# One copy per value tile and per turned attention tile, a state step that stores no minimum, and a new written order

## The chip, the cores and the metric

The kernel runs on one core of one Trainium2 chip. The metric is the device time of one execution in microseconds (us). The kernel before took 319.63 us (median of 3 runs, 318.43 to 320.39).

## The reference

Two stages follow each other. The first is a linear recurrence with decay over 4 batches, 8 heads, 768 steps and head size 48. With a state of 48 x 48 per head, each step computes

```
y[t]  = r[t] @ (state + outer(u*k[t], v[t]))
state = w[t][:, None]*state + outer(k[t], v[t])
```

The heads' outputs side by side are rows x of 384 numbers. The second stage takes them through four experts (E = 4, head size 64). Each expert is causal attention over the 768 positions of a batch (`q = x@wq`, `k = x@wk`, `v = x@wv`, softmax of `0.125*q@k.T`), followed by its own output matrix `wo`. Gate logits `x@w_gate` choose two experts per position, and their outputs are added with softmax weights of the two logits.

## The kernel before, in words

The work is cut into 8 units: batch b = 0..3, half g = 0..1 of the positions (384 each). For every unit there is a recurrence part (`rwkv`) and an attention part (`moe`).

**Recurrence.** The positions are cut into chunks of 64, six per half, and the heads into four pairs p. Scans on VectorE form the products of decays, elementwise work on VectorE and GpSimd (POOL) scales k and r, and TensorE makes all sums in a chunk. What joins the chunks is the state step: `grow` (L435 to L449) computes for chunk c `ys[c+1] = (increment + ys[c]) * decay`, 112 partitions x 48 columns. The increment is in PSUM; the decay is one number per partition. The steps of one pair p form a chain of five or six. Two pairs are handled together (except in the very first unit), so the written order can alternate two chains. The step with chunk index 5 writes `wend` by a plain addition (L441), and for g = 0 the first step is a scaling (L447, L449). The other 144 steps use one VectorE instruction that adds, scales and also takes a minimum over the columns. That minimum goes to a tile `least` of one column, which every step shares and nothing reads:

```
nc.vector.tensor_tensor_reduce(out=new, in0=inc, in1=old, scale=by,
    scalar=3.0e38, op0=ALU.add, op1=ALU.min, accum_out=least[0:112])
```

**Attention.** `proj` makes queries and keys (L696 and L703), `vproj` makes for each 128 positions a row block of 260 columns in one PSUM bank (L735, L741): 128 value columns for experts 0 and 1, 128 for experts 2 and 3, and 4 gate logits. Three copies take these out: to `v_sb0`, to `v_sb1` and to `lg`. `scores` makes masked scores (L808), a row minimum of their negative on VectorE (L819) and exp on ScalarE (L824). `transposes` turns each attention row tile by TensorE, in 128 x 128 blocks, into two PSUM banks. The turned tile of position block ii (0 to 5 in a batch) has ii+1 blocks. The first four go to a tile `ATa` and a fifth and sixth to a tile `ATb`, so the tiles with ii = 4 and 5 are taken out by two copies (helper `copy`, L255 on ScalarE and L257 on VectorE). `attend` multiplies them with the values (L866), `weigh` scales by the gates, and `project_out` applies `wo` (L934) and stores.

**Order.** Nothing is scheduled at run time. The function `rwkv_moe` adds some 2,150 operations to a list, each with the engines that can do it. `ORDER` is a written list of engine letter and operation number (A ScalarE, V VectorE, P TensorE, G GpSimd, S the queue that issues all DMAs, SP); each engine runs its own entries in that order. Waits follow from the tiles that operations really read and write. [...] `P5` to `P98` are matmuls on zeros that fill TensorE at the start; 33 of them are in the list. TensorE runs in four tilings. Full 128-row matmuls (modes F and N) are one, 64 x 64 quarters (Q: recurrence) another, 64 rows (S and T: scores, transposes) a third and 64 columns (V: attention times values) the fourth. A transpose in mode T is two half blocks; where the entry ahead was a full matmul it is done as one full block instead (N).

Of the kernel before, what the change touches and what calls it, by code (L numbers as in the profile page):

```python
# [10 lines left out]

F32 = mybir.dt.float32
# [10 lines left out]
NT = S // 128  # L23
# [187 lines left out]
def rwkv_moe(ctx: ExitStack, tc: tile.TileContext, wkr, wkr0, vY, nat, uN, uT,  # L211
# [78 lines left out]
    least = cst.tile([128, 1], F32, name="least")  # L290
# [36 lines left out]
    def weights(n, src, cols, parts=1):  # L327

        f = sb([128, cols], F32, "ATa", f"w_{n}")
# [14 lines left out]
    def rwkv(b, g, v0, v1):  # L344
# [54 lines left out]
        def keys(group, n):  # L399
# [24 lines left out]
            for x, (p, kt, kts, vn, na, suf, sfv, ys) in enumerate(group):  # L424
# [10 lines left out]
                for c in range(NH - g):  # L435
                    i, a = divmod(c, 2)

                    def grow(e, c=c, o=columns(x, a, i), end=end, ys=ys, sfv=sfv):
# [5 lines left out]
                        if g or c:  # L444
                            nc.vector.tensor_tensor_reduce(out=new, in0=inc, in1=old, scale=by, scalar=3.0e38, op0=ALU.add, op1=ALU.min, accum_out=least[0:112])  # L445
# [214 lines left out]
    def moe(b, g, v0, v1):  # L660
# [6 lines left out]
        if g == 0:  # L667
# [3 lines left out]
            BT["v"] = [sb([128, NT, 128], F32, f"v_sb{ep}", f"v_sb{b}{ep}") for ep in range(2)]  # L671
# [4 lines left out]
        lg = sb([128, 3, E], F32, "lg", f"lg{n0}")  # L676
# [49 lines left out]
        def vproj(i):  # L726
            vp = bank(1, f"vp{n0}{i}")
            o = slice(i * 128, (i + 1) * 128)
            for k in range(3):
                step(0.333)  # L730
                if first:
# [4 lines left out]
                    plan.add("vproj", {"PE": 440}, mm, [(xh, kk) for kk in range(3)] + [wf] + ([vp] if k else []), [vp], claim=v_sb)  # L736
# [5 lines left out]
                plan.add("vproj", {"PE": 356}, mm, [(x_, kk) for x_ in (xh, xl) for kk in range(3)] + [("wh", "vg", 0), ("wl", "vg", 0)] + ([vp] if k else []), [vp],  # L742
                         claim=v_sb)
            for ep in range(2):
                plan.add("v", evac(128), lambda e, ep=ep: copy(e, v_sb[ep]()[:, 3 * g + i, :], vp()[:, ep * 128:ep * 128 + 128]),
                         [vp], [(v_sb[ep], 3 * g + i)])
            plan.add("lg", {"DVE": 70, "ACT": 100}, lambda e: copy(e, lg()[:, i, :], vp()[:, 256:260]), [vp], [(lg, i)])

        def gates():
# [5 lines left out]
            lgk = [(lg, i) for i in range(3)]  # L755
# [74 lines left out]
        def transposes(AT, a, x, i):  # L830
# [6 lines left out]
            plan.add("tp", {"PE": 62 * (ii + 1)}, tr, [a], [tp], mode="T", alt=109 * (ii + 1), claim=AT[0:1 + ii // 4])  # L837
            for j0 in range(0, ii + 1, 4):
                nj = min(4, ii + 1 - j0)

                def ev(e, j0=j0, nj=nj):
                    src = turned(tp, ii + 1)[:, j0:j0 + nj]
                    if j0 == 4:
                        dst = AT[1]()[:, (ii - 4) * 128:(ii - 4 + nj) * 128].rearrange("p (j h c) -> p j h c", j=nj, h=2)
                    else:
                        dst = AT[0]()[:, j0:j0 + nj, i * 128:(i + 1) * 128].rearrange("p j (h c) -> p j h c", h=2)
                    copy(e, dst, src)
                plan.add("ev", evac(nj * 128), ev, [tp], [(AT[j0 // 4], i)])
# [5 lines left out]
        def attend(ep, ATs, i0, i1):  # L854
# [3 lines left out]
            for j in range(nj):  # L858
# [3 lines left out]
                def mm(e, j=j, ia=ia, lo=lo, hi=hi):  # L862
                    for e in range(2):
                        at = ATs[e][j // 4]()
                        at = at[:, j, lo:hi] if j < 4 else at[:, lo - 128:hi - 128] if j == 4 else at[:, 256:384]
                        nc.tensor.matmul(yp()[e * 64:e * 64 + 64, lo:hi], v_sb[ep]()[:, j, e * 64:e * 64 + 64],  # L866
# [3 lines left out]
                         [(v_sb[ep], j)] + [(ATs[e][jj], i) for e in range(2) for i in range(i0, i1) for jj in range(g + 1)  # L870
                                            if 3 * g + i >= jj * 4] + ([yp] if j else []), [yp], mode="V")
# [70 lines left out]
        for ep in range(2):  # L942
            for qk in range(2):
                proj(ep, qk)
            if ep == 0:
                for i in range(3):
                    vproj(i)
                gates()
            ATs = [(sb([128, 4, 384], F32, "ATa", f"ATa{n0}{ep}{e}"),
                    sb([128, 384], F32, "ATb", f"ATb{n0}{ep}{e}") if g else None) for e in range(2)]  # L950
# [49 lines left out]
    for o in plan.order(dict(PE=7200.0 - 216 * WARM[0], DVE=3000.0, ACT=1700.0, POOL=3000.0, SP=1800.0)):  # L1000
# [11 lines left out]
        if e in BOTH and o["kind"] in BOTH[e]:  # L1012
# [10 lines left out]
BUFS = dict(lt=4, nat=3, ys=4, vy=3, suf=4, w2=3, pre=4, am=4, kt=4, rk=2, kts=4, xn=2, xh=2, xl=2, lg=2, asum=2, ge=2, m1=2, rank=2, c1=1, c2=1,  # L1023
            gs=2, mx=6, a=5, gg=2, gT=2, g3=2, yr=2, yh0=1, yh1=1, yl0=1, yl1=1, ob=3, v_sb0=1, v_sb1=1, ATa=3, ATb=2,
# [15 lines left out]
V327 A313 S287 V1082 V1093 G103 V1091 G356 V322 V328 V323 V329 V324 A1094 V330 V284 A314 S403 P1099 P1097 P1064 V283 P1060 G335  # L1040
A1083 P1070 A1085 V368 V1102 V1100 P1065 A1063 P1086 V374 V359 A0 P1071 A1062 A1061 A1101 P1066 P1072 V375 A1103 V406 V369 A1074 V357
V1075 P1088 A1067 V358 A1092 A1089 A1068 A1069 A1087 S480 V373 P336 A1098 V407 G360 A1073 V338 S465 P1104 V337 P1095 A1105 V106 P1106
P345 A1096 V1076 A1107 P378 A346 P342 A343 P394 V347 V344 G1077 S404 A379 A380 V395 V397 A361 G411 A1078 S107 G420 G413 P1108
P381 V376 P339 P1119 V1120 P1109 A340 V1122 V341 A377 V1079 S418 V421 V408 V472 A388 A1121 P1110 P1128 P1137 V1138 A382 V389 V1131
P1175 A1149 P1176 G414 P1179 A362 V383 S365 P1124 V1129 V390 P1177 P1180 V384 A1132 V391 A1178 V422 P1181 S466 P1183 G1080 V392 A1130
P1184 G425 G468 A1125 P1133 G412 A1182 A108 V1140 A1123 V385 V386 V393 V387 V423 P1206 P1135 V428 A1136 A1141 V424 V488 S534 A1134
P1185 V469 V427 V483 G429 G426 A1139 A1187 V1207 S350 P1215 P1243 V415 G474 V1216 A1208 P1142 P1244 A1188 V1218 P1189 A1186 P1195 V1151
V470 A1143 A1217 G476 P1126 P432 P1245 A1219 P1190 V1127 P1191 P448 V484 V471 A434 V487 V473 A433 V1209 V485 G1152 G489 V451 A1246
P435 V449 A1194 P399 A416 V436 G109 V442 V437 V400 V438 A430 V443 S481 V401 A1193 V439 V444 P1153 S519 V440 S419 P1144 A1192
V445 V441 A1154 V446 A1145 V447 A431 G537 G475 A1210 P1196 P1197 P1155 P1226 V1156 V1227 P1223 A1157 A1224 V1229 P1146 P1147 A1198 G477  # L1050
A505 A1200 P1148 P1220 A1199 G1158 A1225 V542 A499 S582 V486 V491 A1230 V538 V490 V522 A1150 V541 P495 V523 A496 P1247 A497 V1201
# [152 lines left out]
```

## Time and profile before

| | us |
|---|---|
| median of 3 runs | 319.63 |
| profiled execution | 319.12 |
| its span, first to last instruction | 317.3 |
| PE (TensorE) busy | 305.6 |
| DVE (VectorE) busy | 271.8 |
| ACT (ScalarE) busy | 243.1 |
| POOL (GpSimd) busy | 127.1 |

Sums below are made against the profiled execution of 319.12 us; 1.8 us of it lie around its span, and it is 0.5 us below the median of the runs. In the rows, PE is matmuls, PEld the loads of weights into TensorE, L12 a line of the kernel before. Matmuls overlap, so that a busy PE can still be waiting for part of the time.

### The profile page before, as it was taken

What the parts mean: (1) busy time and instruction counts of PE and PEld (TensorE: products, weight loads), DVE (VectorE), ACT (ScalarE), POOL (GpSimd) and SP (SyncE); (2) the same over time, 40 slices, a digit from 0 to 9 for tenths busy, and PEclk for the clock granted to TensorE, in tenths of its full rate; (3) what the DMA queues carried; (4) which work ended last, traced back from release to release, by engine and by line L of the source; (5) the groups of instructions that cost most, each with busy time, mean ns of one, the idle gap of its engine ahead of it and who ended that gap; (6) DMA issues with size and microseconds to landing.
All of it is one profiled execution on the core that took longest, in us unless ns stands there. A gap on an engine that the chain in (4) does not pass through costs nothing.

```text
span 317.3 us, 13468 instructions
## 1 busy us (share of the span) xinstructions
PE 305.6 (96%) x5304; PEld 248.4 (78%) x5304; DVE 271.8 (86%) x1001; ACT 243.1 (77%) x881; POOL 127.1 (40%) x252
## 2 busy tenths in 40 slices
PE   6979999999999999999999999999999999999995
PEld 2657667788776998898788978799889977888684
DVE  6999899999999999989998989998778766567852
ACT  1568978999899999998898786577678536677852
POOL 2123433567345454745656843475321010130330
PEclk9999999999999999999999999999999999999999
DMA  7998983762767466677166382341001002001012
GB/s 253 276 244 239 240 222 94 206 172 65 177 185 171 131 197 151 192 178 184 37 169 195 112 208 65 96 141 48 2 27 50 4 0 76 0 27 53 4 50 99
DMA packets 17759, 39.98 MB, mean 126 GB/s; under 512 B 2592, under 2 KB 10528, under 8 KB 17696
## 3 DMA queue, kind: packets, MB, share of 16 engines
q1 hardware_dynamic: 17696, 39.13, 44.7%
q8 instruction: 41, 0.67, 0.9%
q14 instruction: 22, 0.18, 0.2%
HBM read 34.40 MB, written 4.72 MB: 123 GB/s over the span
## 4 chain that ended last, share of the span: by engine, by line
PE 80%; DVE 11%; DMA 4%; issue 2%; ACT 1%; POOL 1%; SPq 0%; DVEq 0%; POOLq 0%; ACTq 0%
PE ps L703 14%; PE ps L808 12%; PE ps L866 11%; PE ps L934 8%; PE ps L251 7%; PE ps L741 7%; PE ps L247 5%; PE ps L613 4%; PE ps L376 3%; PE ps L422 3%; PE ps L378 3%; DMA nat<-in_nat_dram 2%; DVE ys L445 2%; DMA lt<-in_wkr_dram 2%; PE ps L735 1%
## 5 line engine op out<-in xcount | busy, mean ns | idle before, releaser
L824 ACT ACTIVATE a<-a,mx 128x128 f32<-128x128 f32 (+5 forms) x96 | 64.4, 673 | 4.9 <-DVE mx L819 4.3
L819 DVE CUSTOM_DVE_ANT_0 a<-ps,causal 128x256 f32<-128x256 f32 (+5 forms) x96 | 57.6, 619 | 11.7 <-PE ps L808 6.3
L445 DVE CUSTOM_DVE_ANT_0 ys<-ps,ys,suf 112x48 f32<-112x48 f32 x144 | 37.9, 263 | 4.0 <-DVE least L445 0.5
L255 ACT COPY ATa<-ps 128x512 f32<-128x512 f32 (+3 forms) x69 | 32.5, 484 | 11.5 <-PE ps L251 9.6
L866 PE MATMUL ps<-ATa,v_sb 128*64 128x384 f32 (+2 forms) x240 | 35.2, 430 | 0.0
L586 ACT ACTIVATE xn<-nat,rk 128x48 f32<-128x48 f32 x132 | 32.0, 331 | 0.1
L808 PE MATMUL ps<-K,Q 64*128 64x384 f32 (+4 forms) x160 | 31.7, 421 | 0.4 <-DVE xn L396 0.4
L703 PE MATMUL ps<-xh,wh_qk 128*128 128x384 f32 x84 | 31.9, 380 | 0.0
L703 PE MATMUL ps<-xl,wh_qk 128*128 128x384 f32 x84 | 28.4, 338 | 0.0
L703 PE MATMUL ps<-xh,wl_qk 128*128 128x384 f32 x84 | 28.3, 337 | 0.0
L866 PEld LDWEIGHTS ps<-ATa,v_sb 128*64 128x64 f32 x240 | 15.3, 136 | 12.7 <-issue 9.9
L251 PEld LDWEIGHTS ps<-ident,a 64*128 64x128 f32 x492 | 20.7, 138 | 5.6 <-issue 1.1
L376 PE MATMUL ps<-vy,am 64*64 64x48 f32 x768 | 24.8, 219 | 0.1
L378 PE MATMUL ps<-ys,pre 64*64 64x48 f32 (+1 forms) x704 | 24.4, 219 | 0.1
L251 PE MATMUL ps<-ident,a 64*128 64x64 f32 x492 | 23.9, 226 | 0.3 <-DVE least L445 0.2
L255 ACT COPY kts<-ps 128x384 f32<-128x384 f32 x30 | 13.6, 483 | 12.6 <-PE ps L247 9.1
L378 PEld LDWEIGHTS ps<-ys,pre 64*64 64x64 f32 (+1 forms) x704 | 21.9, 134 | 1.7 <-ACT xn L586 0.5
L558 POOL TENSOR_TENSOR kt<-lt,suf 128x384 f32<-128x384 f32 x21 | 19.6, 939 | 8.0 <-DVE w L551 3.8
L376 PEld LDWEIGHTS ps<-vy,am 64*64 64x64 f32 x768 | 22.6, 134 | 0.2 <-DVE am L618 0.2
L808 PEld LDWEIGHTS ps<-K,Q 64*128 64x128 f32 x160 | 15.5, 186 | 7.3 <-issue 2.7
L577 ACT ACTIVATE nat<-nat 128x48 f32<-128x48 f32 x90 | 20.6, 240 | 0.1
L554 POOL TENSOR_TENSOR lt<-lt 128x192 f32<-128x192 f32 x14 | 7.9, 561 | 31.3 <-DVE suf L547 14.9
(164 smaller groups left out, 933.9 us busy)
## 6 DMA issues: line engine op xcount, KB each, us to landing
lt<-in_wkr_dram SPq DMA_DIRECT2D x56, 218.6 KB, 4.5
nat<-in_nat_dram SPq DMA_DIRECT2D x28, 432.0 KB, 4.0
vy<-in_vY_dram SPq DMA_DIRECT2D x32, 144.0 KB, 3.6
out_dram<-ob SPq DMA_DIRECT2D x24, 192.0 KB, 1.9
lt<-in_wkr_dram SPq DMA_DIRECT2D x3, 583.0 KB, 6.0
w_qk<-in_wqk_dram SPq DMA_DIRECT2D x1, 768.0 KB, 8.1
nat<-in_nat_dram SPq DMA_DIRECT2D x4, 144.0 KB, 5.6
w_vg<-in_wvg_dram SPq DMA_DIRECT2D x1, 390.0 KB, 6.5
```

Source lines behind the costliest of these rows:

```text
L251: nc.tensor.transpose(o()[:, h * 512 + i * 64:h * 512 + i * 64 + 64], src[r], ident[r, r])
L255: nc.scalar.copy(o, i)
L376: nc.tensor.matmul(to, am()[k, c, :], vy()[k, c, :], start=zero and x == 0, stop=not first and i == 2 and x == len(group) - 1)
L378: nc.tensor.matmul(to, pre()[r, c, 0:C], ys()[r, c, :], start=i == x == 0, stop=False)
L445: nc.vector.tensor_tensor_reduce(out=new, in0=inc, in1=old, scale=by, scalar=3.0e38, op0=ALU.add, op1=ALU.min, accum_out=least[0:112])
L586: nc.scalar.mul(xn()[:, i, (2 * p + h) * D:(2 * p + h + 1) * D], v()[:, i, h, :], rk()[:, i, h:h + 1])
L703: nc.tensor.matmul(pp()[:, 0:384], w[:, qk, k, cs], x()[:, k, :], start=(k == j == 0), stop=(k == j == 2))
L808: nc.tensor.matmul(spv(x)[:, h, :], q_()[p, t], flat(k_())[p, o], start=j == 0, stop=j == len(terms) - 1)
L819: nc.vector.tensor_tensor_reduce(out=a()[:, 0:n].rearrange("p (a n) -> p a n", a=np_), in0=spv(x), in1=causal[:, S - n:S].rearrange("p (a ...
L824: plan.add("exp", {"ACT": t_exp(n)}, lambda e, x=x, y=y, mx=mx, a=a: nc.scalar.activation(a()[:, 0:n], a()[:, 0:n], AF.Exp, bias=mx(), sca ...
L866: nc.tensor.matmul(yp()[e * 64:e * 64 + 64, lo:hi], v_sb[ep]()[:, j, e * 64:e * 64 + 64], at, start=(j == 0), stop=(j == nj - 1))
L934: nc.tensor.matmul(op()[:, 0:DM], y()[:, t], w[:, ep, :], start=(j + ep == 0), stop=(j == 2 and ep == 1))
```

## The change

Four edits are made. The state step is written as the same VectorE instruction without an output for its minimum, and the tile `least` goes. `v_sb0`, `v_sb1` and `lg` become one tile `v_sb` of 6 x 260 columns with one buffer, filled by one copy of 260 columns per 128 positions; the logits are read from its last 4 columns. `ATa` (3 buffers) and `ATb` (2) become one tile `AT` of 6 x 384 columns with 3 buffers, filled by one copy per turned tile, of up to 768 columns. An attention product of key block j now waits only for the turned tiles that it reads. The list has 80 operations fewer for that, and `ORDER` is written anew from end to end (1,985 entries, 2,067 before).

```diff
-            nc.vector.tensor_tensor_reduce(out=new, in0=inc, in1=old, scale=by, scalar=3.0e38, op0=ALU.add, op1=ALU.min, accum_out=least[0:112])
+            nc.vector._custom_dve(TENSOR_TENSOR_REDUCE_ADD_MIN, out=new, in0=inc, in1=old, s0=3.0e38, s1=by)
...
-            BT["v"] = [sb([128, NT, 128], F32, f"v_sb{ep}", f"v_sb{b}{ep}") for ep in range(2)]
+            BT["v"] = sb([128, NT, 260], F32, "v_sb", f"v_sb{b}")
...
-            for ep in range(2):
-                plan.add("v", evac(128), lambda e, ep=ep: copy(e, v_sb[ep]()[:, 3 * g + i, :], vp()[:, ep * 128:ep * 128 + 128]),
-                         [vp], [(v_sb[ep], 3 * g + i)])
-            plan.add("lg", {"DVE": 70, "ACT": 100}, lambda e: copy(e, lg()[:, i, :], vp()[:, 256:260]), [vp], [(lg, i)])
+            plan.add("v", evac(260), lambda e: copy(e, v_sb()[:, 3 * g + i, :], vp()[:, 0:260]), [vp], [(v_sb, 3 * g + i)])
...
-            for j0 in range(0, ii + 1, 4):
-                nj = min(4, ii + 1 - j0)
...
-                plan.add("ev", evac(nj * 128), ev, [tp], [(AT[j0 // 4], i)])
+            plan.add("ev", evac(ii * 128 + 128), lambda e: copy(
+                e, AT()[:, 0:ii + 1, i * 128:(i + 1) * 128].rearrange("p j (h c) -> p j h c", h=2), turned(tp, ii + 1)), [tp], [(AT, i)])
...
-                         [(v_sb[ep], j)] + [(ATs[e][jj], i) for e in range(2) for i in range(i0, i1) for jj in range(g + 1)
-                                            if 3 * g + i >= jj * 4] + ([yp] if j else []), [yp], mode="V")
+                         [(v_sb, j)] + [(ATs[e], i) for e in range(2) for i in range(ia, i1)] + ([yp] if j else []), [yp], mode="V")
...
 ORDER = """
-V2 S110 S111 V117 V1 V118 V119 V120 V114 V121 V122 S135 V123 V138 V124 V141 V146 S3 V145 S168 V142 V171 S136 P33
...
+S110 V2 V1 S111 S3 P18 P24 S135 V117 V118 S192 V119 S136 V114 V120 V121 V122 V123 V124 V138
...
```

## Rows read from the trace of the kernel before

**Rows 1.** The page: busy time, share of the span and instructions of each engine.

```profile
PE 305.6 (96%) x5304; PEld 248.4 (78%) x5304; DVE 271.8 (86%) x1001; ACT 243.1 (77%) x881; POOL 127.1 (40%) x252
```

**Rows 2.** Three stretches: us, busy us of each engine, clock, DMA share, GB/s.

```profile
0.00:48.00 48.00, 41.36 (x865) 27.86 (x867) 42.75 (x169) 31.23 (x132) 14.24 (x29) 1.00 0.90 245
48.00:160.00 112.00, 110.59 (x2171) 92.41 (x2172) 107.61 (x431) 103.63 (x419) 59.72 (x106) 1.00 0.59 154
160.00:317.30 157.30, 153.62 (x2281) 128.16 (x2277) 121.39 (x403) 108.22 (x333) 53.10 (x118) 1.00 0.23 70
```

**Rows 3.** The page: the chain that ended last, share of the span.

```profile
PE 80%; DVE 11%; DMA 4%; issue 2%; ACT 1%; POOL 1%; SPq 0%; DVEq 0%; POOLq 0%; ACTq 0%
```

**Rows 4.** The chain in order of time, 136 to 158 us: start, us, what.

```profile
145.30 0.47 DVE Kl L723
...
145.82 0.40 PE ps L251 x5
```

**Rows 5.** VectorE in order of time, 140 us: start, us, instruction.

```profile
140.49 0.27 DVE L445 CUSTOM_DVE_ANT_0 ys<-ps,ys,suf 112x48 f32<-112x48 f32 x1 [0.50 <-DVE least L445]
140.68 0.08 DVE L445 DVE_READ_ACCUMULATOR2_ANT least<- 112x1 f32 x1
140.80 0.27 DVE L445 CUSTOM_DVE_ANT_0 ys<-ps,ys,suf 112x48 f32<-112x48 f32 x1
```

**Rows 6.** VectorE in order of time, 219 us.

```profile
219.12 0.26 DVE L445 CUSTOM_DVE_ANT_0 ys<-ps,ys,suf 112x48 f32<-112x48 f32 x1
219.31 0.16 DVE L762 TENSOR_REDUCE m<-lg 128x3 f32<-128x12 f32 x1
219.39 0.20 DVE L763 TENSOR_TENSOR c<-lg 128x48 f32<-128x48 f32 x1
219.50 0.20 DVE L764 TENSOR_TENSOR c<-lg 128x48 f32<-128x48 f32 x1
```

**Rows 7.** Groups of VectorE instructions: count, busy us, mean ns, idle before.

```profile
L445 DVE CUSTOM_DVE_ANT_0 ys<-ps,ys,suf 112x48 f32<-112x48 f32 x144 | 37.9, 263 | 4.0 <-DVE least L445 0.5 <-PE ps L422 0.3
L445 DVE DVE_READ_ACCUMULATOR2_ANT least<- 112x1 f32 x144 | 12.0, 83 | 0.0
```

**Rows 8.** Waits of the weight loader after 48 us: us, times, longest.

```profile
PEld ps L251 <- DVE least L445: 0.9, 3, 0.5
PEld ps L251 <- ACT xn L586: 0.8, 1, 0.8
...
PEld ps L808 <- ACT v_sb L255: 0.2, 1, 0.2
...
PEld ps L808 <- DVE mx L819: 0.2, 1, 0.2
```

**Rows 9.** TensorE in order of time after a run of transposes, 303 us.

```profile
303.16 0.45 PE L934 MATMUL ps<-wh_o,yh 128*128 128x384 f32 x1
303.45 0.34 PE L934 MATMUL ps<-wl_o,yh 128*128 128x384 f32 x1
303.63 0.33 PE L934 MATMUL ps<-wh_o,yl 128*128 128x384 f32 x1
```

**Rows 10.** Copies out of PSUM by shape: count, busy us, mean ns.

```profile
L255 ACT COPY ATa<-ps 128x512 f32<-128x512 f32 x33 | 19.1, 595 | 6.8 <-PE ps L251 5.5 <-DVE mx L819 1.2
...
L257 DVE COPY ATa<-ps 128x512 f32<-128x512 f32 x15 | 10.2, 686 | 2.1 <-PE ps L251 2.0
...
L255 ACT COPY v_sb<-ps 128x128 f32<-128x128 f32 x38 | 9.4, 272 | 3.4 <-PE ps L741 1.9 <-DVE v_sb L257 1.0 <-PE ps L735 0.4
...
L255 ACT COPY ATa<-ps 128x384 f32<-128x384 f32 x12 | 5.8, 486 | 1.5 <-PE ps L251 0.9 <-PE ps L247 0.5
...
L255 ACT COPY ATb<-ps 128x256 f32<-128x256 f32 x11 | 4.2, 383 | 0.5 <-PE ps L251 0.5
...
L257 DVE COPY ATa<-ps 128x384 f32<-128x384 f32 x4 | 2.2, 552 | 1.2 <-PE ps L251 1.2
```

**Rows 11.** The chain in order of time, 0 to 60 us.

```profile
34.40 7.60 DMA nat<-in_nat_dram
```

More of the change, by code (lines that the diff above doesn't have):

```diff
@@ L10 @@
 from concourse._compat import with_exitstack
+from concourse.dve_ops import TENSOR_TENSOR_REDUCE_ADD_MIN
 F32 = mybir.dt.float32
@@ L289, in rwkv_moe @@
     wend = [cst.tile([128, D], F32, name=f"wend{p}") for p in range(NP)]
-    least = cst.tile([128, 1], F32, name="least")
     u_sb = cst.tile([128, DM], F32, name="u_sb")
@@ L327, in weights @@
     def weights(n, src, cols, parts=1):
-        f = sb([128, cols], F32, "ATa", f"w_{n}")
+        f = sb([128, cols], F32, "AT", f"w_{n}")
         h = cst.tile([128, cols], F32R, name=f"wh_{n}")
@@ L735, in mm @@
                         nc.tensor.matmul(vp()[:, 0:260], xh()[:, k, o], wf()[:, k * 260:k * 260 + 260], start=k == 0, stop=k == 2)
-                    plan.add("vproj", {"PE": 440}, mm, [(xh, kk) for kk in range(3)] + [wf] + ([vp] if k else []), [vp], claim=v_sb)
+                    plan.add("vproj", {"PE": 440}, mm, [(xh, kk) for kk in range(3)] + [wf] + ([vp] if k else []), [vp], claim=[v_sb])
                     continue
@@ L754, in gates @@
             c2 = sb([128, 3, E, E], F32, "c2", f"c2{n0}")
-            lgk = [(lg, i) for i in range(3)]
+            lgk = [(v_sb, 3 * g + i) for i in range(3)]
             V = nc.gpsimd
@@ L836, in tr @@
                     turn(e, tp, j, a()[:, j * 128:(j + 1) * 128])
-            plan.add("tp", {"PE": 62 * (ii + 1)}, tr, [a], [tp], mode="T", alt=109 * (ii + 1), claim=AT[0:1 + ii // 4])
-            for j0 in range(0, ii + 1, 4):
-                nj = min(4, ii + 1 - j0)
[L841 to L847, printed above, removed]
-                plan.add("ev", evac(nj * 128), ev, [tp], [(AT[j0 // 4], i)])
+            plan.add("tp", {"PE": 62 * (ii + 1)}, tr, [a], [tp], mode="T", alt=109 * (ii + 1), claim=[AT])
+            plan.add("ev", evac(ii * 128 + 128), lambda e: copy(
+                e, AT()[:, 0:ii + 1, i * 128:(i + 1) * 128].rearrange("p j (h c) -> p j h c", h=2), turned(tp, ii + 1)), [tp], [(AT, i)])
         last = (b, g) == (B - 1, 1)
@@ L863, in mm @@
                     for e in range(2):
-                        at = ATs[e][j // 4]()
-                        at = at[:, j, lo:hi] if j < 4 else at[:, lo - 128:hi - 128] if j == 4 else at[:, 256:384]
-                        nc.tensor.matmul(yp()[e * 64:e * 64 + 64, lo:hi], v_sb[ep]()[:, j, e * 64:e * 64 + 64],
+                        at = ATs[e]()[:, j, lo:hi]
+                        nc.tensor.matmul(yp()[e * 64:e * 64 + 64, lo:hi], v_sb()[:, j, ep * 128 + e * 64:ep * 128 + e * 64 + 64],
                                          at, start=(j == 0), stop=(j == nj - 1))
@@ L948, in moe @@
                 gates()
-            ATs = [(sb([128, 4, 384], F32, "ATa", f"ATa{n0}{ep}{e}"),
-                    sb([128, 384], F32, "ATb", f"ATb{n0}{ep}{e}") if g else None) for e in range(2)]
+            ATs = [sb([128, NT, 384], F32, "AT", f"AT{n0}{ep}{e}") for e in range(2)]
             for i in (1, 0, 2) if last and ep else range(3):
@@ L1114 @@
-P2124 A2125 S2126
+S110 V2 V1 S111 S3 P18 P24 S135 S112 S168 P25 P35 V117 V118 S192 V119 S136 V114 V120 V121 V122 V123 V124 V138
+V141 V146 P30 P36 V142 S113 V145 V171 V143 V147 P9 V144 V174 S169 P16 P11 P23 P115 A116 P22 P13 P12 P17 P28
+P29 V148 P32 S4 V178 S246 S137 P33 P126 A127 P5 V198 P150 V175 S231 A151 V179 P139 P152 A153 V199 P128 V195 A129
+V176 A140 S232 V130 V154 P159 V131 G180 P27 P14 P21 P8 P31 V155 V162 S99 V132 V156 G202 V133 A125 V177 V249 G181
+V157 P19 A149 P183 V134 V158 P37 P15 P7 P10 V160 A184 P6 P185 V200 S193 V250 A186 V234 V201 S285 V238 V203 V204
@@ new lines @@
+V235 V242 P172 V205 P166 V187 A173 S170 S194 P164 P207 G239 V236 A167 V188 V189 V253 S300 V240 V243 A0 V237 V190 G254
+A165 P225 A208 P20 P209 A265 S247 A100 A210 A226 V251 V211 P216 A244 A182 V191 A271 V252 V288 V292 V289 V212 V213 P196
+G255 A197 V217 V219 V214 G241 V290 V215 V293 V294 V303 S286 P1105 S363 V256 S248 V308 V304 P26 P1109 P221 V307 V291 P261
+V257 A206 V296 V258 A222 A263 G101 S104 A262 P227 P223 G309 P264 S348 V266 A228 G295 A224 V272 V267 V268 P277 P229 A245
+V305 V273 V269 A230 V280 V274 V278 V270 S287 S301 S402 A319 A259 V275 V276 V297 V306 V351 V366 A102 V310 V352 A260 P1106
@@ new lines @@
+A1159 P1199 A1200 P1201 A1202 S651 P1244 A1167 V1245 A1237 P1217 S535 A1218 G593 S467 V1247 P1162 A1163 V540 V600 A559 V605 V594 P1240
+A1239 P1253 V1254 A1191 G542 A1248 P549 G530 V1256 A1246 V1192 A551 V604 A550 V544 V601 A1255 V545 G531 P1221 P1222 P1223 P459 S636
+G606 A460 A1241 P462 P456 A457 V461 A463 A1257 P1224 P1225 P1226 V458 P552 G1193 P565 V464 P516 V532 V560 V587 V566 S584 P1294
+A533 V546 V588 V654 G592 V595 A568 V602 V554 V561 G591 V518 A547 G639 S598 S536 P1351 A1268 V562 G569 V555 V556 V563 V517
@@ new lines @@
+V557 A548 V1270 V558 V564 P1299 V603 P1352 P1295 P1300 V640 V643 P1296 S699 V607 P1301 A1297 P612 S637 A1302 P1242 V608 A614 P1251
+A613 P1353 P615 A1243 V1298 P628 V1303 G658 A1252 G1271 V616 S714 V622 A1354 G609 V617 G659 A631 V623 P570 V618 G644 P1260 V624
+V619 V625 V620 S599 V626 V621 A596 V627 V629 V1355 G645 V571 S652 P1321 V572 V641 V655 P1356 P1272 V642 G660 A1261 P1357 P576
+A1273 P573 P1258 P1274 A577 V1324 V1322 P1358 V578 A574 V575 A1259 A1359 V1275 G632 P1249 V656 G717 V1360 P666 V646 P579 A1250 A668
@@ new lines @@
+P633 V657 V647 V661 A667 V718 V702 V662 S653 P669 A610 S753 V703 P682 A611 V663 V704 S700 V664 G648 V634 V635 V683 A670
+A580 V581 A685 P1262 P1263 G686 P1264 P1265 P1266 V676 A665 S638 V705 G721 V677 S715 P1267 G722 P1330 G723 S768 V671 V678 P1339
+V719 P1477 A1323 A1269 P1427 G710 V1342 V679 V1331 G706 V672 A649 V1340 G707 V680 P1417 P1428 P1278 V673 V681 A1332 V1279 P1429 P1435
+P1478 A1430 V674 P1436 V675 V720 P1418 P1479 P1437 A739 P1326 S1168 V708 V756 A650 P729 V724 A1341 A1327 V1333 V709 V711 V725 A730
@@ L1115 @@
+V2063 V2040 P2064 P2065 A2041 A2066 S2067 V2037 V2042 P2047 P2048 A2049 S2050 P2043 P2044 A2045 S2046
 """
```

154 lines of the change are left out of this document (65 added, 89 removed).

## The prediction, made before the result was known

> **What bounds the kernel now.** I read the busy times first. TensorE (PE) is busy for 305.6 of 317.3 us and VectorE (DVE) for 271.8 [rows 1]. The stretches show where that changes [rows 2]. Up to 48 us the DMA engines are 0.90 busy and TensorE works only 41.36 us. From 48 to 160 us TensorE (110.59 of 112), VectorE (107.61) and ScalarE (ACT, 103.63) are all nearly full. After 160 us only TensorE is. So a gain has to shorten TensorE's own list, or remove what it waits for in the first half. A busy PE hides waits, since matmuls overlap; the chain that ended last shows them better: 80% of it is TensorE, 11% VectorE, 4% DMA [rows 3]. One such place is the stretch before 145.8 us, where the transposes at 145.82 follow VectorE's work on the keys' low part at 145.30 [rows 4]. VectorE was late there, and the next view says why.
>
> At 140 us VectorE runs ten state steps of L445 one after the other, each like the three rows shown [rows 5]. The second starts 0.31 us after the first (140.49 to 140.80). By the written order these ten belong to two pairs of heads in turn, so most need nothing of the step ahead of them. What they share is `least`: every step writes it, so every step waits until the one ahead has written it. The row names that releaser. At 219.12 a step is followed by an instruction that shares nothing with it, and that one starts after 0.19 us [rows 6], when the read of the minimum starts too. The dead time is thus the shared tile's, not the arithmetic's.
>
> **The change part by part.** *State step.* The 144 reads of the minimum go (0.083 us each, 12.0 us busy in all) [rows 7], and with them the wait on `least`. In the written order 98 of the 160 steps (16 of them plain additions) are followed at once by a step, 73 times by one of another pair. Two alternating chains then take 0.31 us for two steps instead of 0.62: 73 x 0.155 = 11.3 us of VectorE's time. A step followed by something else frees the engine after 0.19 us now. Without the read I bound that by 0.19 above and 0.11 below (two 48-column instructions, 219.39 to 219.50) [rows 6] and take 0.12, being the same width: 62 x 0.07 = 4.3 us. Together up to 15.6 us of VectorE's time, nearly all before 220 us.
>
> [...] The step at 219.12 lasts 0.26 us and the next instruction starts after 0.19 [rows 6]; independent steps can overlap. [...]
>
> What TensorE gets of this is less. Its weight loader's visible waits after 48 us that end on VectorE are 13 rows, 0.9 to 0.2 us each, 5.9 us in all; those that end on ScalarE are 17 rows, 0.8 to 0.2, 5.6 us in all [rows 8]. They bound the gain from above, zero from below. Of the VectorE part I take half, since a wait that goes uncovers the next one: -3.0 us. After that ScalarE is late next, then the loads.
>
> *Value copies.* Per value tile three copies (two like the 0.272 us one, and a small one) become one of 260 columns, near the 0.383 us of 256 [rows 10]. For 24 tiles that is at least 24 x (0.54 - 0.38) = 3.9 us, mostly on ScalarE. The written list of ScalarE falls from 472 to 413 entries, VectorE's from 718 to 700. The one tile with one buffer adds a wait: the first value copy of a batch has to wait for the last attention product of the batch before. Behind it on ScalarE stand exp and copies, and TensorE waits for those. But the second half of the values already waited for that product in the old list, and the new list puts the projections as far behind it as the old one (25, 23 and 6 TensorE operations; 32, 19 and 5 in the old). I cost it at nothing; without that cover it is one copy, about 0.4 us, three times.
>
> *Turned tiles.* 32 of 96 tiles lose their second copy. On ScalarE one copy of 768 columns comes to 0.595 + 2 x 0.109 = 0.81 us (step from 384 to 512 columns), against 0.595 and 0.383 in a row; on VectorE to 0.686 + 2 x 0.134 = 0.95 [rows 10]. Where the two copies ran on two engines at once, 10 tiles, the turned tile is complete 0.13 us later on ScalarE; and in the new list 7 of the 32 are VectorE's. That is at most 10 x 0.13 + 7 x 0.27 = 3.2 us of lateness; few waits of TensorE name these copies, so I take +0.5. Both sorts of copies make ScalarE lighter by about a tenth of its list, and of its 5.6 us of waits I take 0.8: -0.8 us. Looser waits of attention products, and one more buffer for the fifth and sixth blocks, I cost at nothing: their cover is the other products in the queue.
>
> *Written order.* It is the old one rearranged locally: each unit's first projection, scores and output matrix stand within four TensorE entries of where they stood. I counted tiling changes of TensorE along both lists: 152 before, 141 after. One costs about 0.1 us: the first matmul after transposes holds TensorE from 303.16 to 303.45, the next one 0.18 us [rows 9]. 11 x 0.1 = -1.1 us, wholly on the path. Blocks turned whole fall from 153 to 146; below 0.3 us, left out.
>
> *Loads.* Nine data loads instead of eight now stand ahead of TensorE's first real work, and most of them behind fewer zero matmuls. But the DMA engines are already 0.90 busy up to 48 us [rows 2], and the load that the chain waits for longest, the last natural tile of the second unit (7.60 us from its issue at 34.40) [rows 11], has the same bytes ahead of it in both lists. The bounds are a tenth of the 48 us (-4.8) and a tile's delay of 1.8 us (rival 3). Being DMA-bound lies nearest: -0.3 us.
>
> Sum: -1.1 - 3.0 - 0.8 - 0.3 + 0.5 = -4.7 us, so 319.1 - 4.7 = 314.4 for an execution like the profiled one. The median of the runs is 0.5 above it: **314.9 us**.
>
> **The rivals.** (1) *TensorE's own pace is the bound.* VectorE gets its time back but TensorE waits elsewhere, as its 110.59 of 112 busy us suggest [rows 2]. Only the tiling changes are left: 319.6 - 1.1 = 318.5. The mechanism of the step that overlaps no more than its duration belongs here: 73 x (0.31 - 0.26) = 3.7 us of VectorE's time instead of 15.6, and at the same yield (3.0 of 15.6) 0.7 us for TensorE, so 317.8. [...] Chance 0.26.
>
> (2) *VectorE was the real bound up to 160 us.* It is 96% busy there [rows 2], and every late product may come from it. Then both sums of waits go by three quarters: 0.75 x 11.5 = 8.6, with the tiling 9.7: 319.6 - 9.7 = 309.9. Against it speaks that the chain after 160 us is TensorE's. Chance 0.15.
>
> (3) *A load comes too late at the start: slower.* The new list issues the state inputs of the second unit's last pair ahead of the natural tile of its second pair, and some value tiles later. At 245 GB/s [rows 2] a tile of some 437 KB takes 1.8 us. If two stand ahead of one that TensorE needs, its first matmuls of that unit start 3.6 us later and all behind them too: 319.6 + 3.6 - 1.1 = 322.1. It decides if that load lands after the sums of its pair are reached, as the load of rows 11 does today. Chance 0.11.
>
> That the step is still done with the read, so that nothing changes, I give no chance of its own: the call passes no output for it.
>
> **How the numbers follow.** My forecast has 0.48. Faster or slower by 1% is about what a measurement of this kernel tells from no change: 316.4 and 322.8 us. Forecast and rival 2 lie below: 0.63 faster, with 0.02 for a rival 1 that comes out lower: 0.65. The rest of rival 1 (0.24) and the milder third of rival 3 (0.04) lie between: 0.28. Slower: 0.07. The range 309.9 to 318.6 holds the forecast with its bounds (half or all of the 5.9 us and 5.6 us), nearly all of rival 1 and half of rival 2.
>
> **What would show it.** In the changed trace: no read of a minimum at L445's successor and alternating steps about 0.155 us apart; if they are 0.26 apart, rival 1's mechanism holds. VectorE's busy time from 48 to 160 us clearly below 107.6, ScalarE's below 103.6, and the waits of rows 8 on VectorE about halved. If VectorE has room there and TensorE's stretch still ends at the same time, rival 1 is right. The first attention matmuls at the same time as now show the start unchanged; later ones with a DMA as releaser show rival 3. The forecast is wrong if new waits for the longer copies of turned tiles appear in the first half.

## The result and the profile after

The changed kernel takes 316.69 us (median of 20 runs, 314.4 to 320.24) against 319.77 us of the kernel before beside it (20 runs, 317.69 to 322.19). The ratio is 0.9888, 95% interval 0.9865 to 0.9911: faster by 1.1%. Measured again later on one chip with three experiments, it is 0.9899 (0.9844 to 0.9953). The forecast was 314.9 us, 1.5% faster than before. The profiled execution of the changed kernel took 314.93 us with a span of 312.4 us, at the low end of its runs, so its 4.2 us below the profiled execution of before flatter it by about 1 us.

The page, busy time of each engine, answers to [rows 1]:

```profile
PE 300.6 (96%) x5309; PEld 246.8 (79%) x5311; DVE 267.2 (86%) x841; ACT 237.0 (76%) x826; POOL 123.1 (39%) x247
```

The three stretches, columns as in [rows 2]:

```profile
0.00:48.00 48.00, 40.83 (x896) 28.75 (x899) 42.83 (x145) 32.66 (x143) 15.41 (x28) 1.00 0.86 236
48.00:160.00 112.00, 111.33 (x2212) 94.68 (x2212) 106.70 (x352) 101.52 (x388) 59.94 (x111) 1.00 0.62 165
160.00:312.40 152.40, 148.46 (x2204) 123.41 (x2202) 117.70 (x346) 102.85 (x298) 47.76 (x110) 1.00 0.22 66
```

From 48 to 160 us VectorE executes 352 instructions instead of 431 and is busy for almost as long. Its busy time over the span falls by only 4.6 us, though 144 reads of 0.083 us are gone. The time freed hardly shows there: reads and steps already lay over each other [rows 5], and an overlap is counted once. It shows in the group of the steps, and in how much of the chain that ended last is steps. These are the lines that answer to [rows 3] and [rows 7]; a group of reads no longer exists.

```profile
PE 82%; DMA 6%; DVE 6%; ACT 3%; issue 2%; SPq 0%; POOL 0%; ACTq 0%; POOLq 0%
```

```profile
L445 DVE CUSTOM_DVE_ANT_0 ys<-ps,ys,suf 112x48 f32<-112x48 f32 x144 | 31.2, 258 | 1.0 <-ACT ys L447 0.4
```

VectorE's share of this chain is 6% instead of 11%, but the share proves little: in a second profile of the changed kernel it is 10%, and behind the first 55 us VectorE holds 17.6 us of the chain before and 17.9 after. What went out of the chain are the state steps: 7.3 us of them before, 1.6 and 1.7 in the two profiles of the changed kernel, 2.6 and 0.4 in those of the step alone. The step still lasts 258 ns, but 144 of them cover 31.2 us and not 144 x 0.258 = 37.2: steps now overlap each other. The idle time before them went from 4.0 to 1.0 us.

The weight loader's waits after 48 us, as in [rows 8] (us in total, times, longest):

```profile
PEld ps L922 <- ACT xn L586: 0.8, 1, 0.8
...
PEld ps L252 <- DVE lt L554: 0.6, 1, 0.6
PEld ps L252 <- ACT AT L256: 0.6, 3, 0.2
...
PEld ps L807 <- ACT AT L256: 0.5, 2, 0.3
```

The waits that ended on `least` are gone (the 0.9 us of [rows 8] and two smaller rows, 1.5 in all). All rows that end on VectorE come to 3.4 us, 4.4 in the second profile (before 6.3; the prediction's 5.9 left out two rows of 0.2), those on ScalarE to 4.3 and 4.2 (before 5.6). Waits for copies of turned tiles, which were to show the forecast wrong if they grew, come to 2.0 us on both engines together (before 2.2). The chain where TensorE stood behind the keys' low part [rows 4] now holds TensorE alone (start, us, what):

```profile
143.63 0.48 PE ps L807 x6
144.11 0.20 PE ps L252 x6
144.31 0.56 PE ps L743 x3
```

### The profile page after: what moved, and what is told of

It reads as the page before. It is cut to its first block, busy times and chain, and to the rows that moved or that the text cites. A ratio compares the mean times of both kernels' runs of the same rounds, so it can differ in the third digit from the quotient of the medians.

```text
span 312.4 us, 13242 instructions
## 1 busy us (share of the span) xinstructions
PE 300.6 (96%) x5309; PEld 246.8 (79%) x5311; DVE 267.2 (86%) x841; ACT 237.0 (76%) x826; POOL 123.1 (39%) x247
## 4 chain that ended last, share of the span: by engine, by line
PE 82%; DMA 6%; DVE 6%; ACT 3%; issue 2%; SPq 0%; POOL 0%; ACTq 0%; POOLq 0%
PE ps L705 15%; PE ps L807 11%; PE ps L855 10%; PE ps L922 8%; PE ps L743 7%; PE ps L252 6%; PE ps L248 5%; DMA vy<-in_vY_dram 4%; PE ps L422 3%; PE ps L613 3%; PE ps L376 3%; PE ps L378 3%; PE ps L698 2%; DMA lt<-in_wkr_dram 2%; ACT xn L586 1%
## 5 line engine op out<-in xcount | busy, mean ns | idle before, releaser
L818 DVE CUSTOM_DVE_ANT_0 a<-ps,causal 128x128 f32<-128x128 f32 (+5 forms) x96 | 57.2, 618 | 11.2 <-PE ps L807 8.2
L256 ACT COPY AT<-ps 128x128 f32<-128x128 f32 (+5 forms) x72 | 37.1, 541 | 14.3 <-PE ps L252 11.2
L855 PE MATMUL ps<-AT,v_sb 128*64 128x384 f32 (+2 forms) x308 | 40.0, 404 | 0.0
L855 PEld LDWEIGHTS ps<-AT,v_sb 128*64 128x64 f32 x308 | 20.2, 137 | 17.0 <-issue 12.8
L445 DVE CUSTOM_DVE_ANT_0 ys<-ps,ys,suf 112x48 f32<-112x48 f32 x144 | 31.2, 258 | 1.0 <-ACT ys L447 0.4
L586 ACT ACTIVATE xn<-nat,rk 128x48 f32<-128x48 f32 x126 | 30.6, 325 | 0.2
L807 PE MATMUL ps<-K,Q 64*128 64x384 f32 (+4 forms) x160 | 30.6, 420 | 0.0
L558 POOL TENSOR_TENSOR kt<-lt,suf 128x384 f32<-128x384 f32 x20 | 18.7, 937 | 23.6 <-DVE nat L528 11.7
L376 PE MATMUL ps<-vy,am 64*64 64x48 f32 x768 | 25.0, 220 | 0.2 <-DMA vy<-in_vY_dram 0.2
L376 PEld LDWEIGHTS ps<-vy,am 64*64 64x64 f32 x768 | 22.9, 134 | 0.2 <-issue 0.2
L577 ACT ACTIVATE nat<-nat 128x48 f32<-128x48 f32 x96 | 21.9, 236 | 0.1
L807 PEld LDWEIGHTS ps<-K,Q 64*128 64x128 f32 x160 | 14.8, 186 | 7.0 <-issue 3.7
L743 PE MATMUL ps<-wh_vg,xh 128*128 128x260 f32 x63 | 19.1, 303 | 0.0
L551 DVE TENSOR_TENSOR_SCAN w<-w,inv_pre 128x198 f32<-128x198 f32 x32 | 18.8, 589 | 0.0
```

The lines of the kernel that those rows point to most:

```text
L256: nc.scalar.copy(o, i)
L376: nc.tensor.matmul(to, am()[k, c, :], vy()[k, c, :], start=zero and x == 0, stop=not first and i == 2 and x == len(group) - 1)
L445: nc.vector._custom_dve(TENSOR_TENSOR_REDUCE_ADD_MIN, out=new, in0=inc, in1=old, s0=3.0e38, s1=by)
L586: nc.scalar.mul(xn()[:, i, (2 * p + h) * D:(2 * p + h + 1) * D], v()[:, i, h, :], rk()[:, i, h:h + 1])
L807: nc.tensor.matmul(spv(x)[:, h, :], q_()[p, t], flat(k_())[p, o], start=j == 0, stop=j == len(terms) - 1)
L818: nc.vector.tensor_tensor_reduce(out=a()[:, 0:n].rearrange("p (a n) -> p a n", a=np_), in0=spv(x), in1=causal[:, S - n:S].rearrange("p (a ...
```

## A ruler for single profiles

Two executions of one kernel differ mostly in the first 60 us: by 1.3 to 3.5 us in the start in the table below, and by 0.4 to 0.7 us in the rest. Up to 48 us the DMA engines are 0.90 busy before and 0.86 in the changed kernel, and loads hold 13.6 and 18.7 us of the first 60 us of the chain that ended last. The granted clock of TensorE differs there as well: over the first 30 us its mean is 1.00 in seven of the fourteen traces and 0.77 to 0.94 in the other seven. So I read in every trace one length that leaves the start out, and in which the granted clock is 1.00 in all fourteen: from the last row of matmuls of L376 in the second unit (the sums of the recurrence) to the start of the last matmul of all. The two rows of before, then of the new step alone, then of the changed kernel:

```profile
54.70 0.29 PE L376 MATMUL ps<-vy,am 64*64 64x48 f32 x8
...
313.61 0.34 PE L934 MATMUL ps<-wh_o,yl 128*128 128x384 f32 x1
```

```profile
55.78 0.30 PE L376 MATMUL ps<-vy,am 64*64 64x48 f32 x8
...
312.36 0.34 PE L934 MATMUL ps<-wh_o,yl 128*128 128x384 f32 x1
```

```profile
52.31 0.33 PE L376 MATMUL ps<-vy,am 64*64 64x48 f32 x8
...
308.63 0.34 PE L922 MATMUL ps<-wh_o,yl 128*128 128x384 f32 x1
```

The rest is 313.61 - 54.70 = 258.9 us before, 256.6 with the step alone and 256.3 in the changed kernel. The changed kernel's profile was thus lucky in its start (52.31), not faster behind it.

Part of the rest repeats still better, its middle: from the first scores of the third unit to the first scores of 320 columns in the last unit. These two rows of the step alone give 279.19 - 116.40 = 162.8 us; the other profile of it gives 162.8 as well:

```profile
116.40 0.31 PE L808 MATMUL ps<-K,Q 64*128 64x128 f32 x2
...
279.19 0.40 PE L808 MATMUL ps<-K,Q 64*128 64x320 f32 x2
```

All traces, one profile each:

| kernel | start, us | rest, us | its middle, us | ratio of the medians to before (95%) |
|---|---|---|---|---|
| before | 54.7 | 258.9 | 164.4 | 1 |
| step alone, first | 57.1 | 256.2 | 162.8 | 0.9909 (0.9871 to 0.9947) |
| step alone, second | 55.8 | 256.6 | 162.8 | 0.9886 (0.9826 to 0.9945) |
| one minimum tile per pair | 55.0 | 256.6 | 162.7 | 0.9935 (0.9899 to 0.9971) |
| order alone | 58.8 | 260.1 | 164.7 | 1.0012 (0.9974 to 1.0050) |
| order and copies, old step | 54.2 | 260.0 | 164.5 | 1.0051 (1.0008 to 1.0095) |
| step and both copies, old order | 53.9 | 260.5 | 165.4 | 1.0013 (0.9973 to 1.0052) |
| step and value copy, old order | 56.9 | 258.5 | 164.5 | 0.9968 (0.9929 to 1.0006) |
| step and turned copy, old order | 54.3 | 257.5 | 163.1 | 0.9887 (0.9840 to 0.9933) |
| step and order, first | 55.3 | 255.6 | 162.4 | 0.9876 (0.9810 to 0.9941) |
| step and order, second | 53.7 | 256.3 | 162.4 | 0.9906 (0.9865 to 0.9947) |
| step, order, turned copy | 55.0 | 256.3 | 162.4 | 0.9901 (0.9857 to 0.9944) |
| changed kernel, first | 52.3 | 256.3 | 163.0 | 0.9888 (0.9865 to 0.9911) |
| changed kernel, second | 55.8 | 256.9 | 162.9 | 0.9899 (0.9844 to 0.9953) |

The three kernels with two profiles agree with themselves within 0.7 us in the rest and 0.1 us in the middle. Against before, rest and ratio agree within 1.4 us in every row but one: step and turned copy is 1.4 us shorter by the rest and 3.6 by the medians.

## The experiments

### The step alone, and everything but the step

The first takes the kernel before and changes one call (the tile `least` goes with it); the second takes the changed kernel and puts the old call and `least` back.

```diff
-nc.vector.tensor_tensor_reduce(out=new, in0=inc, in1=old, scale=by, scalar=3.0e38, op0=ALU.add, op1=ALU.min, accum_out=least[0:112])
+nc.vector._custom_dve(TENSOR_TENSOR_REDUCE_ADD_MIN, out=new, in0=inc, in1=old, s0=3.0e38, s1=by)
```

> The kernel before with the new state step alone (no minimum, no shared tile); copies and written order as before. Theory A (the step gives most): independent steps 0.175 us apart instead of 0.311, 9 to 11 us of VectorE's time, of which TensorE gets 2 to 3 us: ratio to before about 0.992. Theory B (the written order gives it): the old order cannot use the time, ratio 0.999 to 1.001. Theory C (only together): about 0.998.

> The changed kernel with the minimum and its shared tile put back into the state step; merged copies and new order stay. Theory A: loses most of the gain, ratio to before about 0.997, steps 0.311 us apart again. Theory B: keeps it, about 0.989. Theory C: little left, 0.998 to 1.002, since the new order counts on a fast step and puts more of the steps side by side (84 pairs of independent steps instead of 73).

The step alone came to 317.61 us, ratio 0.9909; later, beside the changed kernel, to 316.54 us, 0.9886. All without the step came to 321.35 us, 1.0051. The expectation of the second run:

> The new state step alone, a second time, beside the changed kernel. Theory (the step is nearly the whole gain): 0.989 to 0.992, at most 0.3% above the changed kernel. Rival (order and copies together are worth the 1.4 us predicted for them): 0.993 to 0.995, above the changed kernel by 0.45%.

So the step is the whole gain, and the other three edits without it cost half a per cent. VectorE in order of time, the ten steps that [rows 5] show, in the trace of the step alone:

```profile
139.97 1.93 DVE L445 CUSTOM_DVE_ANT_0 ys<-ps,ys,suf 112x48 f32<-112x48 f32 x10
141.82 0.15 DVE L258 COPY lg<-ps 128x4 f32<-128x4 f32 x1
```

Ten steps hold VectorE from 139.97 to 141.82, 0.185 us each, where the kernel before spent 0.31. With the old call put back into the changed kernel the old pace is there again, 128.36 to 128.68:

```profile
128.36 0.27 DVE L445 CUSTOM_DVE_ANT_0 ys<-ps,ys,suf 112x48 f32<-112x48 f32 x1
128.56 0.08 DVE L445 DVE_READ_ACCUMULATOR2_ANT least<- 112x1 f32 x1
128.68 0.27 DVE L445 CUSTOM_DVE_ANT_0 ys<-ps,ys,suf 112x48 f32<-112x48 f32 x1
```

Sorted by the written order, means from a step's start to the next instruction's start on VectorE are: behind a step of the other pair 0.175 us (before 0.311), behind a step that it depends on 0.296 (0.311), and from a step to something else 0.175 (0.192), in the changed kernel. Summed over all 160 steps, from each start to the next instruction's, it is 41.5 us before and 30.3 in the changed kernel; with the step alone, in the old order with its fewer alternating pairs, 34.8 and 33.3. So the step by itself gives VectorE 6.7 to 8.2 us back.

### One minimum tile per pair

Which part of the step's edit counts, the shared tile or the read? Here the minimum is still taken, read and stored, but each pair of heads has its own tile.

```diff
-    least = cst.tile([128, 1], F32, name="least")
+    least = [cst.tile([128, 1], F32, name=f"least{p}") for p in range(NP)]
...
-... accum_out=least[0:112])
+... accum_out=least[p][0:112])
```

> The kernel before with one change: the minimum is still taken, read and stored, but each pair of heads has a tile of its own for it. If the wait on the shared tile is what the edit of the step removes: independent steps about 0.19 us apart, ratio 0.992 to 0.994. If the read of the minimum (0.083 us each) is what counts: 0.31 us apart still for steps of one pair, others 0.27, ratio 0.998 to 1.000. [...]

317.64 us, 0.9935. VectorE in order of time:

```profile
128.71 0.26 DVE L445 CUSTOM_DVE_ANT_0 ys<-ps,ys,suf 112x48 f32<-112x48 f32 x1
128.89 0.08 DVE L445 DVE_READ_ACCUMULATOR2_ANT least<- 112x1 f32 x1
128.89 0.26 DVE L445 CUSTOM_DVE_ANT_0 ys<-ps,ys,suf 112x48 f32<-112x48 f32 x1
129.08 0.08 DVE L445 DVE_READ_ACCUMULATOR2_ANT least<- 112x1 f32 x1
```

The read of 0.08 us runs beside the next step, which starts at the same moment (128.89). Steps of two pairs are 0.188 us apart in the mean; without the read it is 0.175. The rest is 256.6 us, as with the step alone; the median gives back 0.65% of the 0.9 to 1.1%. So most of the gain, perhaps all, is the wait on the shared tile.

### The order alone

The new order, with the old step and the old copies standing side by side where the new one stands.

```diff
 ORDER = """
-V2 S110 S111 V117 V1 V118 V119 V120 V114 V121 V122 S135 V123 V138 V124 V141 V146 S3 V145 S168 V142 V171 S136 P33
...
+S110 V2 V1 S111 S3 P18 P24 S135 S112 S168 P25 P35 V117 V118 S192 V119 S136 V114 V120 V121 V122 V123 V124 V138
...
```

> The new written order alone: old step with its minimum, old two or three copies side by side where the merged one stands, on its engine. Theory A: the 11 tiling changes fewer, about -1.1 us, ratio 0.996 to 0.998. Theory B: about 0.990. Theory C: 1.000 or above.

320.69 us, 1.0012: nothing. Behind the start it is 1.2 us longer than before (260.1; its one trace is of the longest of its runs, 324.9 us, with the latest start), and the kernel with order and copies 1.1 (260.0). With the step, the order is at par with the old one:

> New state step and new written order, but the old two or three copies (side by side where the merged one stands, on its engine). Theory A (step alone gives the gain; order and copies are near zero together): 0.990. Theory D (the merged copies cost time wherever they stand, as they did in the old order): below the changed kernel, 0.985. Theory E (the new order is written for the merged copies, and pays only with them): 0.995 or above.

> New state step and new order, all copies as before, a second time. Theory (copies taken together are worth nothing, the step and a little of the order carry the gain): 0.986 to 0.990, equal to the changed kernel within 0.3%. Rival (the copies are worth the 0.8 us of the prediction): 0.991 to 0.993, above the changed kernel by 0.25% or more.

The two runs gave 317.4 us (0.9876) and 316.97 us (0.9906), against 0.9909 and 0.9886 of the step alone; the second run falls between its two expectations.

### The copies in the old order

The new step with both copies merged, each at the place and on the engine of the first copy that it replaces; then the value copy alone; then the turned copy alone, at the place of the second.

```diff
+            plan.add("v", evac(260), lambda e: copy(e, v_sb()[:, 3 * g + i, :], vp()[:, 0:260]), [vp], [(v_sb, 3 * g + i)])
...
+            plan.add("ev", evac(ii * 128 + 128), lambda e: copy(
+                e, AT()[:, 0:ii + 1, i * 128:(i + 1) * 128].rearrange("p j (h c) -> p j h c", h=2), turned(tp, ii + 1)), [tp], [(AT, i)])
```

> The old written order with the new step and the merged copies (a merged copy stands where the first of the old ones stood, on that one's engine). Theory A: all but the tiling changes, ratio to before about 0.991. Theory B: 0.998 to 1.000. Theory C: about 0.997.

> Old order, new step, one copy per value tile only. If the one-buffer value tile or its later copy is what cost 1% in the old order with both merged: ratio 1.000. If the turned tiles' long copies cost it: 0.990, as with the step alone (0.991).

> Old order, new step, one copy per turned tile only (a merged copy stands where the second of the old ones stood, on that one's engine). If the long copies hold the two PSUM banks and scores wait for them (the trace with both merged shows 1.5 us of scores waiting for a ScalarE copy of AT late in the kernel): ratio 0.998 to 1.002. If the value tile is the cause: 0.990.

Both: 320.42 us, 1.0013, more than any of the three theories had; value copy 319.44, 0.9968; turned copy 317.26, 0.9887. In the old order the copies eat the gain of the step, and the value copy does most of it: in the middle it adds 1.8 us, the turned copy 0.3, both 2.6. Its place in the trace, ScalarE's row first, then TensorE's:

```profile
142.78 0.38 ACT L256 COPY v_sb<-ps 128x260 f32<-128x260 f32 x1 [0.35 <-PE ps L743]
```

```profile
142.46 0.28 PE L743 MATMUL ps<-wh_vg,xl 128*128 128x260 f32 x1
143.20 0.44 PE L933 MATMUL ps<-wh_o,yh 128*128 128x384 f32 x1 [0.47 <-ACT v_sb L256]
```

The output projection (L933) has no bank of PSUM until the copy of the value tile ends at 143.16; TensorE stands for 0.47 us. The copy is not the slow part: the three copies of the kernel before hold a bank until the last of them, which in the step alone starts at 143.88, after the projection. But the program deals out the banks by the written list (`take` in `Plan.order`), and the one copy stands ahead of the projection in it. By that rule the projection gets the value tile's own bank here and another bank in the step alone, where it follows its value tile after 0.13 us (141.12 to 141.25):

```profile
141.12 0.29 PE L741 MATMUL ps<-wh_vg,xl 128*128 128x260 f32 x1
141.25 0.34 PE L934 MATMUL ps<-wh_o,yh 128*128 128x384 f32 x1
```

With both copies there are more such places. This one is late in the kernel, before scores (L807), in the list of the weight loader's waits after 230 us:

```profile
PEld ps L807 <- ACT AT L256: 1.5, 2, 0.9
```

With the step alone no wait there on such a copy is above 0.2 us. These places are a part of the 4.1 us by which the rest is longer than with the step alone; I have not traced all of it.

### The value copies taken out of the changed kernel again

The changed kernel with the three copies of before, side by side in the new order where the one copy stands.

```diff
-            plan.add("v", evac(260), lambda e: copy(e, v_sb()[:, 3 * g + i, :], vp()[:, 0:260]), [vp], [(v_sb, 3 * g + i)])
+            for ep in range(2):
+                plan.add("v", evac(128), lambda e, ep=ep: copy(e, v_sb[ep]()[:, 3 * g + i, :], vp()[:, ep * 128:ep * 128 + 128]),
+                         [vp], [(v_sb[ep], 3 * g + i)])
+            plan.add("lg", {"DVE": 70, "ACT": 100}, lambda e: copy(e, lg()[:, i, :], vp()[:, 256:260]), [vp], [(lg, i)])
```

> The changed kernel, but with the value tile taken out by three copies as before, side by side in the new order where the one copy stands. Theory (the long value copy costs what the shorter list saves: about 0.6% between the step alone and the step with the value copy): 0.982 to 0.986 of the kernel before, some 1 us below the changed kernel, and the waits of the output projection at 142 us for a bank that a value copy holds are absent. Rival (the value copy is neutral, the earlier difference was spread of the runs): 0.988 to 0.990, the same as the changed kernel.

> The changed kernel beside the others on one chip. Both theories: 0.989 of the kernel before, as at first (0.9865 to 0.9911). If it comes to 0.984 or 0.994, the spread between jobs is as large as the differences that the copies and the order are said to make, and those stay open.

316.99 us, 0.9901, and for the changed kernel beside it 316.69 us, 0.9899. The theory, that a version without the value copy would win 1 us, falls: by the medians the value copy is neutral in the new order. The middle still shows half of it: 162.4 us with the old value copies, in this kernel and in both profiles of step and order, and 163.0 and 162.9 in the changed kernel. The value copy costs 0.5 us there, less than the medians can tell. No kernel tried beats the step alone by more than the spread.

## Why the prediction held, and where its sum did not

**The state step (forecast -3.0).** Right. The rest of the kernel behind its start shrank by 2.3 and 2.7 us, the medians by 3.3 to 3.5 us. Its inner numbers were off: independent steps are 0.175 us apart, not 0.155, and a step followed by something else holds VectorE for 0.175 us, not 0.12, so VectorE got 6.7 and 8.2 us back in the two traces of the step alone, and not 15.6. The bound of 0.11 us from two cheaper instructions of the same width [rows 6] was not the nearest row; the pace of 0.19 at 219.12 in the same group was. The yield to TensorE made up for it, 2.3 to 2.7 us of these instead of 3.0 of 15.6; that two errors cancel is luck. Half of the waits on VectorE was a lucky way to get there: in the trace of the step alone these waits fall only from 6.3 to 5.0 and 5.7 us, those on ScalarE from 5.6 to 4.6 and 4.9, together by 1.3 to 2.3 us, and the time fell by more. Rows of waits are a bound here, not a meter.

**Rival 1** falls in its mechanism: in the changed kernel independent steps are 0.175 us apart, not the 0.26 us that a step lasts. Steps that depend on each other are 0.296 us apart there. The rest of rival 1 falls too: it left only the tiling changes as a gain, and 0.7 us of the step at most, and the step alone brings the whole of it.

**Rival 2** (VectorE the bound up to 160 us, -8.6) falls: 6.7 and 8.2 us of VectorE's time bought 2.7 and 2.3. **Rival 3** (a load too late) can't be seen: the start of the rest lies between 53.9 and 57.1 us in the seven traces with the old order and between 52.3 and 58.8 in the seven with the new one. The -0.3 us for loads is undecided for the same reason. In the changed kernel the chain there passes through another load than in [rows 11]:

```profile
46.42 5.28 DMA vy<-in_vY_dram
```

**The written order (forecast -1.1)** is a term that failed as a whole: the prediction counted tiling changes and nothing else that the order does. From the ruler's start to the first scores of the third unit the new list has 28 changes instead of 34; that takes 60.3 and 60.6 us with the step alone and 59.4 to 60.3 in the five traces with step and order, some 0.5 less, no more than the spread. In the middle it has 79 instead of 81, and 162.4 us instead of 162.8. So about 0.1 us for a change is not refuted, but not shown either, since more than tilings differs, and with the old step the same stretches are longer in the new order (61.7 and 61.9 us instead of 61.3, 164.7 and 164.5 instead of 164.4). And the order loses 0.6 us at the end: from the first scores of 320 columns in the last unit to the last matmul it takes 33.7 or 33.8 us in all seven traces that have it, 33.1 or 33.2 in those with the old order and the old turned copies. (The merged turned copies cost as much there in the old order: 33.7, and 34.4 with both copies.) The place, in the changed kernel, VectorE, then GpSimd, then TensorE:

```profile
294.49 0.92 DVE L871 SCALAR_TENSOR_TENSOR gg<-asum,gs 128x8 f32<-128x8 f32 x1
295.44 0.20 DVE L873 RECIPROCAL gg<-gg 128x8 f32<-128x8 f32 x1
295.68 0.69 DVE L874 TENSOR_TENSOR gg<-gg,ge 128x8 f32<-128x8 f32 x1
296.30 1.41 DVE L258 COPY AT<-ps 128x512 f32<-128x512 f32 x2
```

```profile
294.39 1.97 POOL L911 TENSOR_TENSOR yl<-yr,yh 128x384 fp32r<-128x384 f32 x2 [0.69 <-ACT yh L910]
```

```profile
297.12 0.68 PE L252 MATMUL ps<-ident,a 64*128 64x64 f32 x15 [0.38 <-DVE AT L258]
```

Two operations on eight columns take 0.92 and 0.69 us beside GpSimd's work; the copy behind them is late, and TensorE waits for it. All seven traces with this order show it: the two operations slow (0.86 to 0.93 and 0.69 or 0.70 us) with GpSimd beside them, and a wait of TensorE of 0.29 to 0.38 us. In all seven with the old order, as in the kernel before, the same two take 0.15 or 0.16 and 0.17 us, while GpSimd stands still:

```profile
300.58 0.15 DVE L883 SCALAR_TENSOR_TENSOR gg<-asum,gs 128x8 f32<-128x8 f32 x1
...
301.00 0.17 DVE L886 TENSOR_TENSOR gg<-gg,ge 128x8 f32<-128x8 f32 x1
```

I had read the order for its tilings and its queues, not for what it sets side by side on VectorE and GpSimd. That the rest of the 1.2 us of the order alone comes from such places is not shown.

**The copies (forecast -0.8 and +0.5)** are the other term that failed: together nothing that the medians tell in the new order (a rest of 256.3 and 256.9 us with them, 255.6 and 256.3 without; a middle 0.5 us longer), and a loss in the old one. The sizes were right. Copies by shape in the changed kernel answer to [rows 10]:

```profile
L256 ACT COPY AT<-ps 128x768 f32<-128x768 f32 x13 | 10.4, 801 | 1.6 <-PE ps L252 1.4
L256 ACT COPY AT<-ps 128x640 f32<-128x640 f32 x12 | 8.3, 695 | 2.3 <-PE ps L252 2.2
...
L256 ACT COPY v_sb<-ps 128x260 f32<-128x260 f32 x19 | 6.9, 377 | 6.0 <-PE ps L743 6.0
```

```profile
L258 DVE COPY AT<-ps 128x768 f32<-128x768 f32 x3 | 2.9, 951 | 0.1
```

0.80 and 0.95 us were forecast as 0.81 and 0.95, and 0.377 as 0.38. ScalarE became lighter, 103.63 to 101.52 us from 48 to 160 us, with 414 entries in the list instead of 473 (the prediction says 413 and 472). But the prediction looked for the cost of one value copy at the buffer of `v_sb`, and the one place traced in the old order is elsewhere: at the bank of PSUM, which the list hands on to the next projection.

**The sum.** -1.1, -0.8, +0.5 and -0.3 came together to nothing that can be told from zero: -1.7 of the -4.7 us. What is left, -3.0, gives 319.63 - 3.0 = 316.6 us, and 316.69 was measured. VectorE's busy time "clearly below 107.6" was a wrong sign, since that sum counts overlapping work once: it is 106.70 in the changed kernel and 107.76 in the second trace of the step alone, which is as fast.

## What to carry to other kernels

Look for outputs that nothing reads: a statistic of one column, shared by all steps, can order instructions that have nothing to do with each other, and the releaser in the idle column names it. When an edit makes instructions fewer or an engine lighter, ask which wait ends last there before giving it a price; here only the edit whose wait stood in the chain paid. Compare single profiles from a milestone behind the noisy start, not from zero. A share of the chain in one profile can be the noise of the start.

## What the runs showed of the hardware

- In the changed kernel a state step, a VectorE instruction of 0.26 us on 48 columns, lets an independent instruction start after 0.175 us and a dependent step after 0.296. In the kernel before, where all steps write the same column of statistics, the next step starts after 0.311 us. The read of the statistic, 0.083 us busy, costs 0.013 us where the column isn't shared (0.188 us between steps of two pairs with one minimum tile per pair, against 0.175 without the read).
- In the changed kernel VectorE's instruction at 294.49 ends at 295.41, 0.02 us after the first of two GpSimd operations (294.39 to 295.39). The next one that reads two tiles ends at 296.37, 0.02 us after GpSimd's second (295.35 to 296.35). They take 0.92 and 0.69 us, against 0.15 and 0.17 us in the kernel before, where GpSimd stands still beside them. The reciprocal between them, which reads one tile, took 0.20 us in both kernels, though GpSimd's second operation ran beside it in the changed one. Why these two are held up and the reciprocal is not, no run shows.
